# Query loads of six pairs of heads moved from SP's queue to ScalarE's, under a new order list

## The chip, the cores and the metric

The kernel runs on one core of a Trainium2 chip. The metric is the device time of one execution in microseconds, the median of several runs. A core has five engines that each execute their own instruction stream in order: TensorE (PE; its weight loads are listed as PEld), VectorE (DVE), ScalarE (ACT), GpSimd (POOL) and SyncE (SP). SP computes nothing: it issues DMA transfers. ACT and POOL can issue them too. The streams wait for each other by semaphores.

## The reference

Three layers follow each other. The first is causal attention over 2 batches of 8 heads with 576 positions and a head width of 64, with a bias from a running sum; the second a dense feed-forward layer (512 to 2048 to 512) on the 1152 tokens; the third sends each token to one of eight experts of width 1024.

```python
scores = scale * np.matmul(q, k.transpose(0, 1, 3, 2))
cum = np.cumsum(np.maximum(s, 0.0), axis=-1)
bias = -(cum[:, :, :, None] - cum[:, :, None, :])
scores = np.where(causal, -1000000000.0, scores + np.minimum(bias, 0.0))
attn = np.exp(scores - np.max(scores, axis=-1, keepdims=True))
attn = attn / (np.sum(attn, axis=-1, keepdims=True) + 1e-09)
x = np.matmul(attn, v)                    # then tokens x 512
...
h = x @ w_in
g = h * (1.0 / (1.0 + np.exp(-1.702 * h)))
x = g @ w_out
...
# the third layer: the expert of the largest gate logit, then w1, relu, w2, times its gate weight
```

## The kernel before

Operands are fp32 or are split into a high and a low 16-bit part, so that one product takes several matrix products.

**Pairs of heads.** Attention is done by pairs of heads: pair 0 to 7, called `x_` in the code (four of each batch). Their stages are interleaved with each other and with the beginning of the dense layer. For each pair:

- `qk_load` loads k and q of the two heads (288 KB each) to `kraw0`/`kraw1` and `qraw0`/`qraw1`, by the parity of `x_`, on SP (L630).
- `qk_T` transposes them on PE (L651) in the PSUM bank `MI`; ACT copies the results to `QK0` or `QK1` (L657). Two bias rows come from memory (`cum_d`, L640).
- `unit` goes through five query tiles, t = 0 to 4, with 64, 192, 320, 448 and 576 keys. PE computes scores (L680, the mask at L683; t = 0 is `first`, L694) in one of two PSUM score buffers, `SC0` and `SC1`, in turn. DVE takes the maximum (L724, L727), ACT the exponential to `pexp` (L736). The high part goes to `ph` by a copy (ACT L665 or DVE L667; L703 for t = 0), and POOL subtracts it for the low part (L749, L752). SP then issues a DMA transpose of `ph` to `PT` (L759). Tiles 0 and 1 share one, `PT01`, of 7 blocks of 128; `PT2`, `PT3` and `PT4` have 10, 14 and 18. For the last pair `PT3` and `PT4` are transposed in two halves each. Each of `PT` and `ph` exists once, so that the next pair's work on a tile waits for the last use of it.
- `av_unit` multiplies `PT` with `V` on PE (L779) into `AV`, DVE scales the result, PE transposes it (L803), and ACT (L806) and DVE (L808) write it to `xT`, the input of the dense layer.

**Around them.** Loads of v (L554), of weights of the dense layer (512 KB each to the `wraw` tiles: L320 for w_in, L323 for w_out) and of constants (L544, L545) are issued from SP too. The weights are converted from 64-bit floats on ACT, DVE and POOL (L352 to L369). The dense layer's first product is at L392 and L396 (by `dense`, `mm1`), its second at L425 and L426 (`mm2`). From about 130 us on the kernel computes the dense layer and then the experts.

**What sets the order.** A class `Plan` records operations, each with its engine, a function that emits it and what it depends on. `run` then emits them in the sequence of the table `ORDER`, a list of operation numbers (lines 23 to 133). So each engine's stream is that list, filtered by engine. `QS` maps the names `sp`, `pool`, `act` to the engines whose queues issue DMAs. The numbers of `dma`, `issue` and the like in the recorded operations are a planner's; `op` takes them, and the emission doesn't use them:

```python
        order = [n for n in ORDER if n0 <= n < self.done]
...
        for n in order:
            assert all(d < n0 or place[d] < place[n] for d in self.ops[n][2])
            self.ops[n][1]()
```

Of the kernel before, what the change touches and what calls it, by code (L numbers as in the profile page):

```python
# [198 lines left out]
def fused_kernel(ctx, tc, q, k, v, s, w_in, w_out, w_gate, w1, w2, cap, out):  # L199
    nc = tc.nc  # L200
# [20 lines left out]
    NBLK = 5  # L221
# [74 lines left out]
    QS = {"sp": nc.sync, "pool": nc.gpsimd, "act": nc.scalar}  # L296
    ISS = {"sp": 540.0, "pool": 1100.0, "act": 600.0}
# [176 lines left out]
    pl = Plan()  # L474
# [150 lines left out]
    def qk_load(x_):  # L625
        b, p = divmod(x_, NPR)
        i = x_ % NQR
# [1235 lines left out]
```

## Time and profile before

| | |
|---|---|
| median of 3 runs | 449.59 us (449.38 to 450.73) |
| the profiled execution | 453.84 us, its span 452.1 us |
| mean granted clock of PE over the span | 0.99 of full speed |
| busy share: PE, DVE, ACT, POOL | 94%, 75%, 59%, 28% |

The profile is of one execution, whose time (453.84 us) includes what lies around the span (452.1 us). Its times are counted from the start of the span. A line such as `L680` is a line of the kernel. SP's rows, marked `SPq`, show how long the engine was occupied with issuing a DMA, not how long the transfer took. "Idle before" in square brackets is the time in which an engine waited, and behind the arrow stands what ended that wait.

### The profile page before, as it was taken

How to read it: one execution, taken by the hardware profiler on the slowest of the kernel's cores; microseconds unless marked ns; L12 is line 12 of the kernel's file. 1: busy time of each engine (PE TensorE's matmuls, PEld its weight loads, DVE VectorE, ACT ScalarE, POOL GpSimd, SP SyncE). 2: the span in 40 equal slices, each digit the busy share in tenths (PEclk: the TensorE clock that was granted, in tenths of full speed). 3: DMA queues.
4: the chain of work that ended last, by engine and by line, in shares of the span. 5: the costliest groups of instructions: out<-in, count | busy, mean ns of one | idle time of the engine just before them, and what ended most of it. 6: DMA issues, size and time to landing. Idle time of an engine off the chain costs nothing.

```text
span 452.1 us, 10556 instructions
## 1 busy us (share of the span) xinstructions
PE 424.5 (94%) x3920; PEld 303.3 (67%) x3920; DVE 339.0 (75%) x909; ACT 268.5 (59%) x565; POOL 125.5 (28%) x147
## 2 busy tenths in 40 slices
PE   7878888999899999999999999999899999999992
PEld 6556566777555554555555665557899999999972
DVE  7688687898868787785565674878667778889971
ACT  2597789887344556454434443664355668868840
POOL 4365674687321212121110001500300113112122
PEclk9999999999989999999999999999999999999997
DMA  7899999999983423539900006795768789899901
GB/s 160 216 235 201 193 178 203 223 207 203 186 279 95 154 93 127 187 94 344 327 6 1 2 1 210 276 342 149 268 188 266 254 254 340 308 290 334 315 30 50
DMA packets 98000, 88.04 MB, mean 195 GB/s; under 512 B 65631, under 2 KB 76895, under 8 KB 97926
## 3 DMA queue, kind: packets, MB, share of 16 engines
q1 hardware_dynamic: 96068, 81.76, 67.7%
q0 software_dynamic: 1872, 5.52, 3.3%
q8 instruction: 32, 0.52, 0.5%
q14 instruction: 28, 0.23, 0.2%
HBM read 60.59 MB, written 14.17 MB: 165 GB/s over the span
## 4 chain that ended last, share of the span: by engine, by line
PE 54%; DMA 3%; DVE 2%; issue 2%; ACT 1%; POOL 1%; POOLq 0%; DVEq 0%
PE SC L425 8%; PE MX L392 5%; PE MI L392 4%; PE SC L426 4%; PE AV L1485 3%; PE AV L1486 3%; PE AV L1488 3%; PE MX L396 2%; PE MI L396 2%; PE AV L425 2%; PE MI L1454 2%; PE MI L1459 2%; PE MX L1454 2%; PE MI L1455 2%; PE MX L1459 2%
## 5 line engine op out<-in xcount | busy, mean ns | idle before, releaser
L425 PE MATMUL SC<-woH,gtH 128*128 128x512 f16 x212 | 63.5, 381 | 0.0
L392 PEld LDWEIGHTS <-wiH 128*128 128x128 f16 x384 | 37.7, 99 | 32.2 <-issue 3.2
L680 PE MATMUL SC<-QK 128*128 128x288 f32 (+3 forms) x160 | 52.6, 455 | 6.6 <-ACT pexp L736 5.4
L749 POOL TENSOR_TENSOR ph<-pexp,ph 128x512 f16<-128x512 f32 (+4 forms) x32 | 44.2, 1386 | 13.4 <-DVE ph L667 13.4
L392 PE MATMUL MI<-xT,wiH 128*128 128x384 f16 x216 | 44.2, 331 | 0.2 <-DVE th L402 0.2
L369 POOL TENSOR_TENSOR wiL<-wvi,wiH 128x512 f16<-128x512 f32 x16 | 19.9, 1244 | 87.6 <-ACT wiH L365 87.6
L425 PEld LDWEIGHTS <-gtH 128*128 128x128 f16 x276 | 26.6, 98 | 24.7 <-issue 0.3
L736 ACT ACTIVATE pexp<-SC,smA 128x192 f32<-128x192 f32 (+3 forms) x64 | 34.7, 573 | 12.1 <-DVE smA L724 8.4
L1372 DVE SCALAR_TENSOR_TENSOR woL<-wraw,woH 128x1024 f16<-128x1024 f32 x32 | 38.7, 1220 | 2.8 <-ACT woH L1370 2.8
L426 PE MATMUL SC<-woL,gtH 128*128 128x512 f16 x106 | 40.6, 383 | 0.0
L1372 DVE SCALAR_TENSOR_TENSOR wiL<-wraw,wiH 128x1024 f16<-128x1024 f32 x32 | 38.7, 1218 | 1.5 <-ACT wiH L1370 1.1
L680 PEld LDWEIGHTS SC<-QK 128*128 128x128 f32 x160 | 27.8, 196 | 16.3 <-ACT pexp L736 7.6
L392 PE MATMUL MX<-xT,wiH 128*128 128x384 f16 x168 | 35.1, 326 | 0.8 <-DVE th L402 0.8
L1370 ACT ACTIVATE wiH<-wraw 128x1024 f16<-128x1024 f32 x32 | 33.2, 1056 | 1.7 <-DMA wraw<-in_moe_w_dram 1.4
L1370 ACT ACTIVATE woH<-wraw 128x1024 f16<-128x1024 f32 x32 | 33.4, 1055 | 1.2 <-DMA wraw<-in_moe_w_dram 1.0
L408 DVE SCALAR_TENSOR_TENSOR gtH<-th,gtH 128x384 f16<-128x384 f32 x46 | 26.1, 574 | 10.4 <-ACT gtH L405 10.3
L1523 POOL DMA_INDIRECT out_dram<-x2R,small x9 | 10.7, 1190 | 81.2 <-ACT xT L1469 40.6
L1150 POOL DMA_INDIRECT xs_d<-x2R,small x9 | 10.4, 1150 | 80.9 <-DVE sqr L1245 42.7
L405 ACT ACTIVATE gtH<-th 128x384 f16<-128x384 f32 x46 | 23.3, 516 | 13.5 <-DVE th L402 8.6
L657 ACT ACTIVATE QK<-MI 64x288 f32<-64x288 f32 x57 | 24.3, 427 | 5.8 <-PE MI L651 5.0
L779 PE MATMUL AV<-V,PT 128*128 128x65 f16 (+1 forms) x640 | 23.7, 193 | 4.3 <-DMA PT<-ph 4.1
L396 PEld LDWEIGHTS <-wiL 128*128 128x128 f16 x192 | 18.6, 98 | 12.8
(347 smaller groups left out, 1080.7 us busy)
## 6 DMA issues: line engine op xcount, KB each, us to landing
wraw<-in_moe_w_dram SPq DMA_DIRECT2D x64, 512.0 KB, 5.8
wraw<-in_moe_w_in_dram SPq DMA_DIRECT2D x16, 512.0 KB, 6.5
wraw<-in_moe_w_out_dram SPq DMA_DIRECT2D x16, 512.0 KB, 5.2
xs_d<-x2R SPq DMA_DIRECT2D x16, 257.0 KB, 5.7
kraw<-in_k_dram SPq DMA_DIRECT2D x8, 288.0 KB, 4.9
qraw<-in_q_dram SPq DMA_DIRECT2D x8, 288.0 KB, 3.9
out_dram<-x2R SPq DMA_DIRECT2D x9, 256.0 KB, 7.4
x2R<-xs_d SPq DMA_DIRECT2D x8, 257.0 KB, 3.6
```

The source lines that it names most:

```text
L392: nc.tensor.matmul(ps, lhsT=whi[:, kc], rhs=xT[:, a, kc, cs], start=(kc == 0 and a == 0), stop=False)
L396: nc.tensor.matmul(ps, lhsT=wlo[:, kc], rhs=xT[:, 0, kc, cs], start=False, stop=(kc == KC - 1))
L408: pl.op("dve", t_dve(CN) + 65 * len(sums), lambda: nc.vector.scalar_tensor_tensor(out=gh[:, 1], in0=th, scalar=half, in1=gh[:, 0], op0=ALU ...
L425: nc.tensor.matmul(o, lhsT=gh[:, a, ts], rhs=whi, start=(fc == 0 and a == 0), stop=False)
L426: nc.tensor.matmul(o, lhsT=gh[:, 0, ts], rhs=wlo, start=False, stop=(fc == NFC - 1))
L657: pl.op("act", t_act(3 * TQ, False) + 130, lambda o=o, in_=in_, sc=sc: nc.scalar.activation(out=o, in_=in_, func=AF.Copy, scale=sc), r=[bk ...
L680: nc.tensor.matmul(o, lhsT=t_[:, 2 * r, i0:i0 + rows], rhs=t_[:, 2 * r + 1, j0:j0 + n], start=True, stop=(j0 + n <= i0))
L736: pl.op("act", t_act(wdt, False, 1), lambda o=o, e=e, r=r, nm=nm: nc.scalar.activation(out=e, in_=o, func=AF.Exp, bias=nm[:rows, r:r + 1]) ...
L749: pl.op(eng, (t_pool if eng == "pool" else t_dve)(n * T_), lambda rs_=rs_, e_=e_: e_.tensor_tensor(out=hl[:, rs_, 0:T_], in0=pe[:rows, rs_ ...
L779: nc.tensor.matmul(av[:, slot, r, 0:D + 1 - h_], lhsT=PT[t][:, r * (1 + 2 * t) + pb, :] if t else PTf[:, 64 * r:64 * r + P], rhs=rhs, star ...
L1370: pl.op("act", t_act(1024), lambda: nc.scalar.activation(out=dhi, in_=raw, func=AF.Copy, scale=SE), r=[rk], w=kh, rank=rank, after=after)
L1372: pl.op("dve", t_dve(1024) + 65, lambda: nc.vector.scalar_tensor_tensor(out=dlo, in0=raw, scalar=SE, in1=dhi, op0=ALU.mult, op1=ALU.subtra ...
```

## The change

In `qk_load` the loads of q for pairs 2 to 7 (the third to the eighth) are issued by ACT's queue. Those of k, and of q for pairs 0 and 1, stay on SP. The table `ORDER` is replaced by another one over the same operation numbers, which changes the streams of all engines in many places.

```diff
 ORDER = [
-    0, 2, 6, 8, 1, 7, 23, 13, 9, 3, 21, 4, 22, 14, 5, 29, 12, 19, 32, 20, 35, 33, 38, 10, 24, 30, 25, 41, 36, 31, 39, 37,
+    0, 1, 6, 15, 2, 8, 7, 21, 13, 9, 3, 22, 4, 23, 12, 5, 29, 20, 32, 19, 35, 33, 24, 38, 30, 34, 11, 25, 10, 41, 36, 31,
...
         for nm, src in (("k", k), ("q", q)):
-            t = raws[nm][i]
-            pl.op("sp", 0, lambda t=t, src=src: nc.sync.dma_start(
+            t, eng = raws[nm][i], "act" if x_ > 1 and nm == "q" else "sp"
+            pl.op(eng, 0, lambda t=t, src=src, eng=eng: QS[eng].dma_start(
                 out=t[:TQ], in_=src[b, 2 * p:2 * p + 2].rearrange("r (p c) d -> p r c d", c=S // TQ)),
-                w=[("raw", nm, i)], dma=820, after=[("vraw", NBLK - 1, 0)] if 1 <= x_ <= 2 else ())
+                w=[("raw", nm, i)], dma=820, issue=ISS[eng], after=[("vraw", NBLK - 1, 0)] if 1 <= x_ <= 2 else ())
```

Three places of the new order follow. In the rows a name such as `qraw0_113` is a tile and its number; the arrow points from source to destination.

ACT, at pair 2 (the copies to `QK1` are those of pair 3's keys and queries). Before:

```order
L657 ACTIVATE QK1_112<-MI_109 64x288 x2
L736 ACTIVATE pexp2_119<-SC0_105,smA_132 128x320 x2
L736 ACTIVATE pexp1_118<-SC1_106,smA_132 128x192
L806 ACTIVATE xT_90<-MX_110 128x320
L736 ACTIVATE pexp1_118<-SC1_106,smA_132 128x192
L657 ACTIVATE QK1_112<-MI_109 64x288 x2
L703 ACTIVATE ph01_122<-pexp0_117 128x64
L665 ACTIVATE ph01_122<-pexp1_118 128x2x192
L365 ACTIVATE wiH0_77<-wvi0_94 128x512
L736 ACTIVATE pexp3_120<-SC1_106,smA_132 128x448 x2
```

After:

```order
L657 ACTIVATE QK1_112<-MI_109 64x288 x2
L630 DMA qraw0_113<-in_q_dram 96x2x384
L736 ACTIVATE pexp1_118<-SC1_106,smA_132 128x192 x2
L665 ACTIVATE ph01_122<-pexp1_118 128x2x192
L657 ACTIVATE QK1_112<-MI_109 64x288
L806 ACTIVATE xT_90<-MX_110 128x320
L657 ACTIVATE QK1_112<-MI_109 64x288
L736 ACTIVATE pexp2_119<-SC0_105,smA_132 128x320 x2
L736 ACTIVATE pexp3_120<-SC1_106,smA_132 128x448
L630 DMA qraw1_114<-in_q_dram 96x2x384
L736 ACTIVATE pexp3_120<-SC1_106,smA_132 128x448
```

Both 192-wide exponentials now stand ahead of the 320-wide ones and of the copy to `xT`, a load of q stands ahead of them (pair 4), and another (pair 5) between the two 448-wide exponentials; the conversion at L365 and the copy at L703 have gone elsewhere.

SP, from the transposes of pair 0's last tile to those of pair 1's. Before:

```order
L630 DMA qraw1_114<-in_q_dram 96x2x384
L630 DMA kraw0_115<-in_k_dram 96x2x384
L759 DMA_TRANSPOSE PT4_129<-ph4_126 128x18x128
L759 DMA_TRANSPOSE PT2_127<-ph2_124 128x10x128
L630 DMA qraw0_113<-in_q_dram 96x2x384
L554 DMA vraw0_136<-in_v_dram 64x8x64 x2
L759 DMA_TRANSPOSE PT01_123<-ph01_122 128x7x128
L320 DMA wraw0_91<-in_moe_w_in_dram 128x4x256
L759 DMA_TRANSPOSE PT3_128<-ph3_125 128x14x128
L640 DMA QK1_112<-cum_d_73 2x2304
L759 DMA_TRANSPOSE PT4_129<-ph4_126 128x18x128
```

After:

```order
L630 DMA kraw0_115<-in_k_dram 96x2x384
L759 DMA_TRANSPOSE PT4_129<-ph4_126 128x18x128
L759 DMA_TRANSPOSE PT2_127<-ph2_124 128x10x128
L554 DMA vraw0_136<-in_v_dram 64x8x64
L759 DMA_TRANSPOSE PT01_123<-ph01_122 128x7x128
L320 DMA wraw0_91<-in_moe_w_in_dram 128x4x256
L640 DMA QK1_112<-cum_d_73 2x2304
L759 DMA_TRANSPOSE PT3_128<-ph3_125 128x14x128
L759 DMA_TRANSPOSE PT4_129<-ph4_126 128x18x128
```

Both loads of q are gone from this stretch, and one of the two pieces of v is issued later.

SP, at the end of the attention: the last rows of pair 6 and those of pair 7. Before:

```order
L759 DMA_TRANSPOSE PT01_123<-ph01_122 128x7x128
L323 DMA wraw1_92<-in_moe_w_out_dram 128x1024
L759 DMA_TRANSPOSE PT2_127<-ph2_124 128x10x128
L759 DMA_TRANSPOSE PT3_128<-ph3_125 128x14x128
L323 DMA wraw0_91<-in_moe_w_out_dram 128x1024
L759 DMA_TRANSPOSE PT4_129<-ph4_126 128x18x128
L759 DMA_TRANSPOSE PT2_127<-ph2_124 128x10x128
L759 DMA_TRANSPOSE PT01_123<-ph01_122 128x7x128
L320 DMA wraw2_93<-in_moe_w_in_dram 128x4x256
L759 DMA_TRANSPOSE PT3_128<-ph3_125 128x7x128 x2
L759 DMA_TRANSPOSE PT4_129<-ph4_126 128x9x128 x2
```

After:

```order
L759 DMA_TRANSPOSE PT4_129<-ph4_126 128x18x128
L323 DMA wraw0_91<-in_moe_w_out_dram 128x1024
L759 DMA_TRANSPOSE PT01_123<-ph01_122 128x7x128
L759 DMA_TRANSPOSE PT2_127<-ph2_124 128x10x128
L323 DMA wraw1_92<-in_moe_w_out_dram 128x1024
L759 DMA_TRANSPOSE PT3_128<-ph3_125 128x14x128
L759 DMA_TRANSPOSE PT4_129<-ph4_126 128x18x128
L759 DMA_TRANSPOSE PT01_123<-ph01_122 128x7x128
L759 DMA_TRANSPOSE PT2_127<-ph2_124 128x10x128
L320 DMA wraw2_93<-in_moe_w_in_dram 128x4x256
L759 DMA_TRANSPOSE PT3_128<-ph3_125 128x7x128 x2
L759 DMA_TRANSPOSE PT4_129<-ph4_126 128x9x128 x2
```

The two weight loads to `wraw0` and `wraw1` stand ahead of pair 6's PT01 and PT3; before, `wraw0` stood between pair 6's PT3 and PT4, and `wraw1` between its PT01 and PT2. Pair 7's PT01 now stands ahead of its PT2.

## Rows read from the trace of the kernel before

**Rows 1.** The page's first part: busy us, share of the span, instructions

```profile
PE 424.5 (94%) x3920; PEld 303.3 (67%) x3920; DVE 339.0 (75%) x909; ACT 268.5 (59%) x565; POOL 125.5 (28%) x147
```

**Rows 2.** Windows: stretch, its length, busy us by engine, granted clock, DMA share, GB/s

```profile
40.00:80.00 40.00, 32.84 (x389) 24.43 (x388) 31.32 (x77) 33.16 (x79) 25.35 (x27) 1.00 1.14 193
120.00:140.00 20.00, 18.13 (x148) 10.12 (x145) 15.48 (x33) 7.61 (x15) 4.07 (x14) 0.91 0.80 206
140.00:320.00 180.00, 178.96 (x1125) 100.52 (x1123) 127.50 (x331) 90.31 (x178) 23.40 (x22) 1.00 0.48 157
```

**Rows 3.** PE's waits: line, releaser, us in total, times, longest

```profile
PE SC L680 <- ACT pexp L736: 5.4, 7, 1.2
PE AV L779 <- DMA PT<-ph: 4.1, 3, 1.9
```

**Rows 4.** Timeline of PE, 42 to 71 us: start, duration, instruction, idle before

```profile
42.12 1.77 PE L680 MATMUL SC<-QK 128*128 128x448 f32 x4 [1.19 <-ACT pexp L736]
...
48.33 0.34 PE L694 MATMUL SC<-QK 128*64 128x64 f32 x4 [0.27 <-ACT xT L806]
...
49.49 0.92 PE L680 MATMUL SC<-QK 128*128 128x192 f32 x4
...
52.41 1.01 PE L779 MATMUL AV<-V,PT 128*128 128x65 f16 x28 [1.89 <-DMA PT<-ph]
...
66.97 0.44 PE L651 MATMUL MI<-identF,qraw 96*128 96x96 f32 x3 [0.79 <-DMA qraw<-in_q_dram]
...
70.21 1.77 PE L680 MATMUL SC<-QK 128*128 128x448 f32 x4 [1.24 <-ACT pexp L736]
```

**Rows 5.** Timeline of SP's issues, 29 to 62 us

```profile
29.75 6.97 SPq L759 DMA_TRANSPOSE PT<-ph  x2
36.81 0.54 SPq L630 DMA_DIRECT2D qraw<-in_q_dram  x1
37.41 1.37 SPq L554 DMA_DIRECT2D vraw<-in_v_dram  x2
...
45.75 3.20 SPq L759 DMA_TRANSPOSE PT<-ph  x1
...
61.35 0.58 SPq L630 DMA_DIRECT2D qraw<-in_q_dram  x1
```

**Rows 6.** Timeline of POOL, the last subtraction for pair 0's PT4

```profile
27.42 0.87 POOL L752 TENSOR_TENSOR ph<-pexp,ph 128x128 f16<-128x128 f32 x1
```

**Rows 7.** Timeline of ACT, 40 to 69 us

```profile
40.17 1.25 ACT L736 ACTIVATE pexp<-SC,smA 128x320 f32<-128x320 f32 x3 [0.76 <-DVE smA L724]
...
68.44 0.26 ACT L703 ACTIVATE ph<-pexp 128x64 f16<-128x64 f32 x1 [1.84 <-DMA PT<-ph]
```

**Rows 8.** Timeline of PE at the end of the attention

```profile
121.36 0.59 PE L425 MATMUL SC<-woH,gtH 128*128 128x512 f16 x2
...
124.04 0.50 PE L779 MATMUL AV<-V,PT 128*128 128x65 f16 x11 [1.87 <-DMA PT<-ph]
```

**Rows 9.** Timeline of SP's issues at the end of the attention

```profile
108.71 0.58 SPq L323 DMA_DIRECT2D wraw<-in_moe_w_out_dram  x1
109.47 4.79 SPq L759 DMA_TRANSPOSE PT<-ph  x1
...
118.07 1.22 SPq L759 DMA_TRANSPOSE PT<-ph  x1
```

**Rows 10.** Timeline of POOL, the subtraction for pair 7's PT3

```profile
114.97 0.91 POOL L749 TENSOR_TENSOR ph<-pexp,ph 128x384 f16<-128x384 f32 x1
```

**Rows 11.** Windows: the six us behind PE's wait at the end of the attention

```profile
124.00:130.00 6.00, 5.96 (x54) 3.42 (x55) 3.18 (x4) 2.56 (x5) 2.75 (x13) 0.72 1.05 301
```

**Rows 12.** Instructions of line L630 for q: duration in ns, least, median, most

```profile
L630 SPq DMA_DIRECT2D qraw<-in_q_dram x8: 444/557/1292, 1.7 to 89.2; - x8
```

**Rows 13.** Timeline of PE at the start of pair 0

```profile
19.20 1.24 PE L680 MATMUL SC<-QK 128*128 128x288 f32 x4 [0.61 <-ACT pexp L736]
...
20.74 0.47 PE L651 MATMUL MI<-identF,qraw 96*128 96x96 f32 x3
```

218 rows, old and new, of the table ORDER are left out of this document.

## The prediction, made before the result was known

> **What bounds the kernel now.** The table of busy times comes first: TensorE (PE) is busy 94% of the span [rows 1], so 452.1 - 424.5 = 27.6 us is all that any reordering can remove without removing work. The table by stage tells where that idle time lies [rows 2]. Between 140 and 320 us PE is busy 178.96 of 180, so whatever is won before 140 us is carried to the end: nothing there waits long enough to absorb it. From 40 to 80 us, inside the attention, PE is idle 40 - 32.84 = 7.16 us, and from 120 to 140 us, where the last pair of heads hands over to the feed-forward layer, 1.87 us, with a granted clock of 0.91. The list of PE's waits says what ends this idle time [rows 3]: the two score buffers, released by ScalarE's exponentials (ACT L736, 5.4 us in 7 waits), and the transposed probabilities that the DMA brings (PT<-ph, 4.1 us in 3 waits). Those are the terms that the change can move. VectorE, GpSimd and the dense part are not read further, since they are late nowhere that matters here.
>
> The profiled execution took 453.84 us (span 452.1); the median of the runs is 449.59. All durations below are of the profiled execution, the difference is formed against 453.84 and then carried to the median.
>
> **The change, part by part.** Six loads of queries (pairs 2 to 7) leave SP's queue and join ScalarE's (ACT's), and the whole order is new. PE executes the same matrix products before and after, so only waits can change.
>
> *a) The stall at pair 1's last transpose.* PE waited 1.89 us at 50.5 for PT4 of pair 1 [rows 4]. SP is the cause to look at: its ten issues from 29.75 to 45.75 follow each other with gaps of 0.2 us at most, direct loads between transposes [rows 5]. The change takes out ahead of that PT4 the q load (0.54 plus a gap of 0.06) and one of the two pieces of v (1.37 / 2 = 0.68). Ahead of pair 0's PT4 it takes out the q load (the row at 29.75 can begin no earlier than its data, and GpSimd finished those at 27.42 + 0.87 = 28.29 [rows 6], so at most 1.46). SP gains 0 to 2.76 us there. But PE reaches PT4 of pair 1 earlier as well, for the scores of pair 3 that stood ahead of it (0.34 + 0.92 [rows 4]) now stand behind: 1.26 us of cover is gone. Net: -1.26 to +1.5. I take 0.1: half of SP's gain (SP is back to back, but the data of its transposes may not all be ready sooner), less the lost cover.
>
> *b) The score buffers at pair 2.* PE waited 1.19 us at 42.12 for the exponentials of the 192-wide unit [rows 4]. On ACT the two 320-wide exponentials of the other buffer stood ahead of the first 192-wide one (the three took 1.25 us together [rows 7]), and the copy to xT ahead of the second. Now both 192-wide ones stand ahead of all that. The gain is 0 to 1.19; I take 1.1, because the two wide exponentials and the copy are together about as long as the wait. The q load that now stands ahead of the exponentials is charged in e).
>
> *c) Pair 3.* PE waited 0.79 us for q of that stage (66.97) and 1.24 us at 70.21 for the score buffer [rows 4]; behind the latter stands ACT's own wait of 1.84 us at L703, which overwrites the source of transpose PT01 of pair 3 and so waits for it until 68.44 [rows 7]. The q load now is issued from ACT while pair 2 is still computed, so the first wait should go. On SP the q load of 0.58 us ahead of that transpose is gone [rows 5], and a load of v is moved behind that transpose. Gain 0 to 2.03; I take 1.2, the larger wait, since part of it will be filled by the next thing that is late (the maximum of VectorE).
>
> *d) The end of the attention.* PE waited 1.87 us until 124.04 for PT3 of pair 7 [rows 8], whose first half was issued at 118.07, so issue to use is 5.97 us [rows 9]. Ahead of it the transpose PT4 of pair 6 took SP 4.79 us; the PT4 at 45.75 took 3.20 [rows 5, 9]. Before it a 512 KB weight load (108.71) stands directly between PT3 and PT4. The new order puts both weight loads ahead of earlier transposes, so I price PT4 at 3.20: 1.59 sooner, plus the load's 0.76 (108.71 to 109.47), 2.35 together. PT3's first half would then start at 115.7 (its data are ready at 115.88 at the latest [rows 10], so 0.2 may be lost) and land at 121.7. PE arrives at 124.04 - 1.87 = 122.17, or 0.59 earlier, since one group of L425 is moved behind: 121.6. The stall falls from 1.87 to about 0.1. Right behind the stall the granted clock fell: 0.72 over 124 to 130 us [rows 11], between the levels of 1.2 and 2.4 GHz, which cost 6 x 0.28 = 1.7 us. PE had waited 1.87 us just before. A wait of 1.89 at 50.5 was not followed by such a fall (1.00 from 40 to 80 us [rows 2]), so that the fall goes with the stall is an assumption. Gain 1.8 + 1.7 = 3.5, bounds 0 to 3.6.
>
> *e) What ACT pays.* No DMA is issued from ACT in the trace of before. The nearest row is the same load issued by SP: 0.444 / 0.557 / 1.292 us for least, median, most [rows 12]. ACT has time to spare (33.16 busy of 40 between 40 and 80 us [rows 2]), but its place in the loop of two score buffers is what PE waits for. Two of the six (pairs 2 and 7) stand beside copies that nobody waits for; four (pairs 3 to 6) stand between or ahead of exponentials or the copies that feed them. 4 x 0.557 = 2.2 us; bounds 0 (all covered by ACT's idle time) to 6 x 1.292 = 7.8. I take 2.2, the median, for it is the same kind of load.
>
> *f) The start.* In the new order the first 288-wide scores of pair 0 (19.20) stand behind the transposes of q of pair 1 (20.74) [rows 13], an operand that comes by DMA. 0.47 us of PE work stands ahead of the chain of exponentials: +0.5, bounds 0 to 1.5 (20.74 - 19.20, if the wait for q is as long as it looks).
>
> *Other moves.* The weight loads of the dense part, the biases and the constants move by a few places on SP, with PE's 7.16 us of idle time as cover; I cost them at nothing, but if that cover is gone each is worth its issue, 0.6 us.
>
> The Trainium skill ("DMA: Bandwidth & Descriptors", section "Issuing engines are not separate DMA queues") says that DMAs from any engine run on the same 16 engines and interleave, and that a second issuing engine saves only the issuing time. By that page the queue move would be worth six times 0.557 = 3.3 us of SP's time and no transfer would be faster. The trace of before cannot bear it out for ACT, since ACT issued no load there. The mechanism it would act by here is rival C.
>
> **The sum.** a) to c) lie on one loop, in which a wait removed at one buffer returns in part at the other; I count half: (0.1 + 1.1 + 1.2) / 2 = 1.2. Then d) 3.5, less e) 2.2, less f) 0.5: 2.0 us gained. 453.84 - 2.0 = 451.8 for a profiled execution; 449.59 - 2.0 = 447.6, rounded to **447.5 us** for the median.
>
> **The rivals.**
> B. *Both gains arrive in full and ACT hides its issues.* ACT's idle time of 6.84 us between 40 and 80 speaks for it [rows 2]. Then a) to c) give 2.4, d) 3.5, e) about 0.6, f) 0.5: 4.8 us, **445** (443.5 to 446).
> C. *The transfers, not the issuing, are the limit, and the change doesn't do what it says.* The DMA share is 1.14 from 40 to 80 us [rows 2], more than the sixteen engines' time by this count, and the issue of a PT4 takes 3.2 to 4.8 us, far longer than a direct load's 0.56, as if it were held by the transfers. If so, taking q off SP leaves the same bytes: PT lands when it did, q takes bandwidth from the transposes in flight, and the 4.79 of d) stays. The gain of a), c) and d) is gone, b) and e) cancel: **449.6** (448.6 to 450.6). Against it: at 109.47 the issue is slow only where a large load is directly ahead.
> D. *Slower: ACT pays.* The issue on ACT stands ahead of the exponentials that release the score buffers, PE waits, and every later exponential is late by as much. It decides from about 0.6 us for each of the six if the end stall stays (six times 0.6 = 3.6 against a gain of 1.2 from a) to c)): 449.59 - 1.2 + 3.6 + f) 0.5 = **452.5**, with 451 to 454 for issues of 0.4 to 0.9. The 1.292 at the top of the rows and the wait of 1.84 that ACT already suffers [rows 7] speak for it; that four of the six have other work before PE needs their exponentials speaks against it.
>
> **How the numbers follow.** The forecast has 0.40, with its own range 446 to 448.6; B 0.15; C 0.20; D 0.25. A measurement of this kernel can tell about 0.3% (1.35 us) from no change. Below 448.2 lie most of the forecast and B: 0.52 faster. Within 448.2 to 450.9 lie C and a little of the forecast's and D's edges: 0.23. Above: 0.25. The range must leave out no more than 2 in 10: from 444.0, inside B, to 451.8, inside D.
>
> **What the profile after would show.** Right: a wait for PT<-ph at the end of the attention under 0.4 us and a granted clock near 1.00 in the 6 us behind it; SP's PT4 of pair 6 near 3.2 us; q loads on ACT of about 0.56 us; PE's waits for L736 below 5 us in all. Wrong in d): PT4 of pair 6 near 4.8 us again, or the clock fallen as before (C). Wrong in e): q issues on ACT near 1.3 us, with PE's waits on L736 grown by 3 us or more (D). Wrong in f): PE's first 288-wide scores later than 20 us by more than 0.7. Any new wait of more than 2 us between 140 and 440 us would upset the carrying of the gain to the end.

## The result, and the profile after

The changed kernel takes 452.4 us (median of 20 runs) against 449.92 for the kernel before in the same comparison (20 runs): a ratio of 1.0053, 95% interval 1.0032 to 1.0074. It is slower by 0.53%, or 2.4 us. The forecast of 447.5 had the wrong sign, and the time lies outside the range.

The profiled execution of the changed kernel took 451.84 us (span 450.1). That this is 2.0 less than the profiled execution before says nothing of the change: that one lay 3.9 us above its own median (453.84 against 449.92), this one 0.6 below. A second profiled execution of the kernel before (run e1 below) took 451.84 too, span 450.1, to the digit the same. So the two kernels are compared below by stretches and by timed ratios, not by the two spans.

The first part of the page, and the table by stage with columns as in [rows 2]; the last stretch is one in which the clock fell:

```profile
PE 422.1 (94%) x3920; PEld 303.0 (67%) x3920; DVE 339.3 (75%) x909; ACT 269.4 (60%) x565; POOL 126.8 (28%) x147
```

```profile
40.00:80.00 40.00, 35.43 (x429) 26.83 (x427) 34.75 (x79) 33.81 (x79) 27.17 (x29) 0.99 1.11 201
120.00:140.00 20.00, 20.00 (x151) 11.33 (x150) 17.18 (x35) 9.51 (x19) 4.59 (x16) 1.00 0.76 204
140.00:320.00 180.00, 177.56 (x1116) 99.84 (x1115) 127.41 (x342) 90.17 (x178) 25.14 (x24) 1.00 0.48 154
30.00:42.00 12.00, 7.60 (x73) 5.68 (x70) 8.20 (x16) 6.01 (x14) 5.14 (x6) 0.72 1.10 198
```

PE's idle time from 40 to 80 us fell from 7.16 to 4.57 us, and that from 120 to 140 us from 1.87 to nothing, with a clock of 1.00 where it was 0.91 [rows 2]. Both were forecast. Two stretches lost. From 140 to 320 us, taken for a stretch that carries every gain to the end, the idle time rose from 1.04 to 2.44 us. And from 30 to 42 us PE was idle 4.4 of 12 us at a clock of 0.72, where the kernel before was idle 2.2 us at 1.00.

PE's waits (columns as in [rows 3]), the largest of the attention and then those behind it:

```profile
PE SC L680 <- ACT pexp L736: 3.1, 6, 1.1
PE AV L779 <- DMA PT<-ph: 2.9, 4, 1.5
PE AV L779 <- DVE V L620: 2.3, 1, 2.3
PE MX L803 <- DVE xT L808: 2.1, 3, 1.4
...
PE SC L1000 <- DVE th L995: 1.2, 2, 1.1
PE MI L983 <- DMA x2R<-xs_d: 0.4, 1, 0.4
```

The two waits of [rows 3] went from 9.5 us in all to 6.0. The third row (the product with V, 2.3 us at 35.93) was 0.2 us before. The last two rows stand at 306 to 320 us, where the kernel selects tokens for the experts (L983, L1000), and the kernel before has neither; it has one of 1.3 us a little later instead (L1454 for DVE's L1470).

### The profile page after: what moved, and what is told of

The parts are those of the page before. It is cut to its first block, busy times and chain, and to the rows that moved or that the text cites. A ratio compares the mean times of both kernels' runs of the same rounds, so it can differ in the third digit from the quotient of the medians.

```text
span 450.1 us, 10568 instructions
## 1 busy us (share of the span) xinstructions
PE 422.1 (94%) x3920; PEld 303.0 (67%) x3920; DVE 339.3 (75%) x909; ACT 269.4 (60%) x565; POOL 126.8 (28%) x147
## 4 chain that ended last, share of the span: by engine, by line
PE 66%; DMA 13%; DVE 7%; ACT 6%; issue 3%; SPq 2%; POOL 1%; POOLq 0%; ACTq 0%; DVEq 0%
PE SC L425 7%; PE MI L392 6%; PE MX L392 4%; PE SC L680 4%; DMA PT<-ph 4%; PE AV L1485 3%; PE SC L426 3%; PE AV L1486 3%; PE AV L1488 3%; DMA wraw<-in_moe_w_dram 3%; PE MI L396 3%; PE AV L425 3%; PE AV L779 2%; DMA x_d<-x2R 2%; PE MX L396 2%
## 5 line engine op out<-in xcount | busy, mean ns | idle before, releaser
L749 POOL TENSOR_TENSOR ph<-pexp,ph 128x512 f16<-128x512 f32 (+4 forms) x32 | 47.3, 1478 | 16.6 <-DVE ph L667 8.4
L736 ACT ACTIVATE pexp<-SC,smA 128x448 f32<-128x448 f32 (+3 forms) x64 | 34.9, 577 | 15.5 <-DVE smA L724 9.8
L369 POOL TENSOR_TENSOR wiL<-wvi,wiH 128x512 f16<-128x512 f32 x16 | 19.6, 1226 | 77.9 <-ACT wiH L365 71.2
L1523 POOL DMA_INDIRECT out_dram<-x2R,small x9 | 11.8, 1310 | 73.1 <-ACT x2R L1566 65.0
L779 PE MATMUL AV<-V,PT 128*128 128x65 f16 (+1 forms) x640 | 24.8, 194 | 5.2 <-DMA PT<-ph 2.9
L779 PEld LDWEIGHTS <-PT 128*128 128x128 f16 x640 | 22.9, 98 | 7.4 <-DMA PT<-ph 3.5
```

The costliest lines, as they stand in the source:

```text
L736: pl.op("act", t_act(wdt, False, 1), lambda o=o, e=e, r=r, nm=nm: nc.scalar.activation(out=e, in_=o, func=AF.Exp, bias=nm[:rows, r:r + 1]) ...
L749: pl.op(eng, (t_pool if eng == "pool" else t_dve)(n * T_), lambda rs_=rs_, e_=e_: e_.tensor_tensor(out=hl[:, rs_, 0:T_], in0=pe[:rows, rs_ ...
L779: nc.tensor.matmul(av[:, slot, r, 0:D + 1 - h_], lhsT=PT[t][:, r * (1 + 2 * t) + pb, :] if t else PTf[:, 64 * r:64 * r + P], rhs=rhs, star ...
```

## The experiments

Sixteen runs were made, in four groups on three chips: e1, e3, e4 and e5; e2, e6, e7 and e8; h1 to h4 on the same chip as the second group; i1 to i4. Each ratio is to the kernel before, run in the same group (medians 451.16, 451.39, 451.36 and 449.62). The interval of a ratio reaches 0.2 to 0.3% to either side, so single ratios that differ by 0.2% are not told apart, and what follows rests on several that agree, or on rows.

**The order against the queue.** e1 is the kernel before again; e2 the changed kernel again. e3 has the queue move under the old order, e4 the new order with all loads of q on SP, e5 the new order with pairs 2 and 3 back on SP.

> The kernel before, unchanged, for a second trace. My sum took the stall of 1.87 us at the end of the attention and the fall of the clock behind it (1.7 us) as if every execution had them; the profiled execution of before took 453.84 us, the median of 20 is 449.92. If the fall of the clock belongs to that execution alone, this trace has a time of 449 to 451 us, a granted clock of 0.99 or more over 120 to 130 us and no loss of more than 0.3 us to the clock there. Rival: it belongs to the kernel, and this trace shows a wait of 1.5 us or more at the end of the attention and a clock of 0.8 to 0.9 over 120 to 130 us, whatever its total.

> The changed kernel, unchanged, for a second trace and as the measure for the next two on this chip. Theory 1 (the changed order and queue make two waits of PE between 30 and 36 us, and the clock falls behind them in most executions): the waits of about 1.5 us for PT and 2.3 us for V (L620) stand here again, SP waits 5 us or more for q at PT2 of pair 0, and the mean granted clock of the runs lies 0.003 to 0.005 under that of before; 451.5 to 453 us. Theory 2 (chance of one execution): the waits or the fall of the clock are not seen again and the mean clock is that of before.

> The old order list, with the six loads of q on ACT's queue: the queue move alone. Theory 1 (what hurts is that SP's transposes wait for the landing of an ACT load, because all hardware DMAs take their completion semaphores in turn from the same eight, so that a DMA waits for the one eight places before it, and ACT's load lands late): here the transpose PT2 of pair 0 comes eight places behind the first of the ACT loads, so SP shows a wait for q there of 1 to 5 us, and the time is 451 to 455. Theory 2 (ACT pays for the issues in the loop of the score buffers): six issues of 0.33 us, 450.5 to 452, and no wait of SP for q. Theory 3 (the new order is what costs, the queue nothing): 449.2 to 450.6.

> The new order list with all loads of q on SP's queue: the order alone. Theory 1: SP's wait of 5.6 us at PT2 of pair 0 is gone, PT2 is issued before 23 us instead of 26.99, PE's waits of 1.48, 0.64 and 2.29 us at 31 to 36 us and the half clock behind them are gone; 445 to 449 us. Theory 2: the six issues of 0.33 us leave ACT, 450 to 451. Theory 3: the order costs as much as with the queue, 451.5 to 453, with the same waits at 31 to 36 us.

> The new order list, loads of q for pairs 2 and 3 back on SP, those for pairs 4 to 7 on ACT. Theory 1: only the first ACT load was eight places ahead of a transpose that was waited for, so this does as well as with all on SP, 445 to 449 us, with no wait of SP for q. Theory 2: four of the six issues remain on ACT, 451 to 452. Theory 3: 451.5 to 453.

```diff
-            t, eng = raws[nm][i], "act" if x_ > 1 and nm == "q" else "sp"
+            t, eng = raws[nm][i], "sp"
```

(This is e4; e5 has `x_ > 3`; e3 has the line of the changed kernel and the old table.)

Measured: e2 1.0047 [1.0027, 1.0067], e3 1.0017 [0.9985, 1.0050], e4 1.0031 [1.0005, 1.0057], e5 1.0020 [0.9989, 1.0052]. The new order loses time even with every load of q on SP, by an interval that excludes no change. The queue move alone is not told from nothing here. So, by these values, most of the loss is not ACT's, against rival D. In e2's trace the wait for V is there again (2.1 us) and SP's wait for q too (3.8), but PE's wait for PT at 31 to 34 us is not. The mean clock of e2's executions is 0.985 where the kernel before has 0.991, a difference that its first theory had nearly so; the section on the prediction comes back to that.

e1 speaks on step d). It took 451.84 us where 449 to 451 was expected, but the clock is what it was run for. Its row at the end of the attention, and two six-us stretches, the second right behind it:

```profile
123.08 0.50 PE L779 MATMUL AV<-V,PT 128*128 128x65 f16 x11 [2.27 <-DMA PT<-ph]
```

```profile
120.00:126.00 6.00, 3.73 (x38) 2.15 (x37) 3.75 (x9) 1.38 (x4) 0.79 (x1) 1.00 1.21 192
126.00:132.00 6.00, 6.00 (x60) 3.86 (x59) 5.31 (x11) 3.06 (x6) 1.96 (x13) 1.00 1.03 387
```

The same program waits 2.27 us there, more than the 1.87 of [rows 8], and the granted clock stays at 1.00. The fall to 0.72 of [rows 11] stands in that one execution and in none of the other seventeen traces.

**Mending what the trace after showed first.** The longest single wait of PE in the trace after is that of the product with V, 2.3 us; e6 moves the last two pieces of V ahead of other work on DVE, e7 does so with e5's queues. e8 is the kernel before with one thing from the new order, the weight loads of step d).

> The changed kernel with one edit on VectorE: the last two low halves of V (L620, from wiL and woL) stand ahead of the cast of pair 1's third tile and of two maxima, instead of behind them. Theory 1: PE's wait of 2.3 us for V at 33 to 36 us goes, the wait for PT remains (SP still waits for q at PT2 of pair 0), and the clock falls there more seldom: 1.5 to 3 us faster than the changed kernel on the same chip. Theory 2 (the wait is only handed on to the score buffers): within 0.7 us of the changed kernel, with a new wait of PE of over 1.5 us between 33 and 45 us.

> The same edit on VectorE, and the loads of q for pairs 2 and 3 back on SP. Theory 1: both waits go (PT2 of pair 0 is issued at about 22 us and the cast of pair 1's third tile no longer waits), 2.5 to 5 us faster than the changed kernel, 447.5 to 450 us; mean clock as in before. Theory 2: within 1 us of the changed kernel.

> The kernel before with one edit on SP: the weight load to wraw0 stands ahead of pair 6's PT01 and the one to wraw1 ahead of its PT3, as in the new order; all other streams are those of before. This is step d) of the prediction alone. If it holds, PT4 of pair 6 takes about 3.2 us instead of 4.8 on SP, PE's wait at the end of the attention falls from 1.9 to 2.4 us to under 0.7, and the time is 1 to 2.5 us less than before. Rival: SP issues without a gap there anyway and the transposes take as long in sum, the wait stays over 1.5 us and the time is that of before within 0.6 us.

e6, on DVE:

```diff
+L620 SCALAR_TENSOR_TENSOR V_130<-wiL_82,misc,V_130 128x8x64
+L620 SCALAR_TENSOR_TENSOR V_130<-woL_86,misc,V_130 128x8x64
 L667 CAST ph_124<-pexp_119 128x2x320
 L724 TENSOR_REDUCE smA<-SC_106 128x2
 L727 TENSOR_REDUCE smA<-SC_105 128x1
-L620 SCALAR_TENSOR_TENSOR V_130<-wiL_82,misc,V_130 128x8x64
-L620 SCALAR_TENSOR_TENSOR V_130<-woL_86,misc,V_130 128x8x64
```

e8, on SP, at pair 6:

```diff
 L759 DMA_TRANSPOSE PT_129<-ph_126 128x18x128
-L759 DMA_TRANSPOSE PT_123<-ph_122 128x7x128
-L323 DMA wraw_92<-in_moe_w_out_dram 128x1024
-L759 DMA_TRANSPOSE PT_127<-ph_124 128x10x128
-L759 DMA_TRANSPOSE PT_128<-ph_125 128x14x128
 L323 DMA wraw_91<-in_moe_w_out_dram 128x1024
+L759 DMA_TRANSPOSE PT_123<-ph_122 128x7x128
+L759 DMA_TRANSPOSE PT_127<-ph_124 128x10x128
+L323 DMA wraw_92<-in_moe_w_out_dram 128x1024
+L759 DMA_TRANSPOSE PT_128<-ph_125 128x14x128
 L759 DMA_TRANSPOSE PT_129<-ph_126 128x18x128
```

Measured: e6 1.0046 [1.0022, 1.0069], e7 1.0032 [1.0005, 1.0060], e8 0.9978 [0.9959, 0.9996]. Moving V forward gains nothing that shows. In e7 the wait for V is gone; in e6, too, but PE there waits for transposes in its place:

```profile
32.65 0.66 PE L779 MATMUL AV<-V,PT 128*128 128x65 f16 x16 [1.75 <-DMA PT<-ph]
34.51 1.38 PE L779 MATMUL AV<-V,PT 128*128 128x65 f16 x22 [0.92 <-DMA PT<-ph]
```

So the largest single wait was no cost that shows by itself; in e6 it was handed on. That theory fell. e8 gains 0.22%, 1.0 us, by an edit of SP's queue alone. PE is busy all of 120 to 130 us in it, at a clock of 1.00. Its PT4 of pair 6:

```profile
107.49 3.33 SPq L759 DMA_TRANSPOSE PT<-ph  x1
```

**Which half of the order loses.** The operations up to about 130 us ("attention") and the rest were put together from different tables. h1: attention of e8, rest of the new order. h2: attention of the new order with q on ACT, rest of the old. h3: as h2 with e7's edits. h4: e8 with the two 192-wide exponentials of pair 2, and the maximum on DVE that they need, ahead of the 320-wide ones: step b) by itself.

> Attention as in the kernel before with its two weight loads early (the run e8), but everything behind it (from about 130 us on: dense layer, routing, experts) in the new order. Theory 1 (the new order loses time behind the attention too: PE waits for the selection matrix, L1000, and for the rows of x2, L983, about 1.6 us together at 306 to 320 us in all traces of the new order and in none of the old): 1 to 2 us slower than e8 and these waits of 1.0 to 1.8 us are in its trace; about that of before, 451 to 452. Theory 2 (these waits are covered by a shorter tail): within 0.6 us of e8, 450 to 450.6.

> The changed kernel's attention (new order, q on ACT) and the rest in the old order. Theory 1: 1 to 2 us faster than the changed kernel, 451 to 452 when before is at 451.3, with no wait at L1000 over 0.3 us; what is left over before is the clock behind the waits at 30 to 36 us. Theory 2: as slow as the changed kernel, 452.8 to 453.6.

> The new attention mended (loads of q for pairs 2 and 3 on SP, the last two halves of V early on VectorE) and the rest in the old order. Theory 1: the gain of the end of the attention remains, the waits at 30 to 36 us and at 306 to 320 us do not: 449.5 to 451. Theory 2 (the new attention costs in other places too): 451.5 to 453.

> The run e8 with step b) of the prediction alone: in pair 2 the 192-wide maximum and exponentials stand ahead of the 320-wide ones on VectorE and ACT. If step b) holds, PE's wait of 1.0 to 1.2 us at 42 us goes and the time is 0.5 to 1.2 us under e8. Rival: the wait is handed on to the next score buffer and the time is that of e8 within 0.4 us.

h1 against e8, on DVE at the selection (many other rows differ too):

```diff
-L995 TENSOR_SCALAR th_89<-iotaW,small 128x128 x2
+L995 TENSOR_SCALAR th_89<-iotaW,small 128x128
+L1127 TENSOR_TENSOR small<-small,SC_106 128x8
 L1143 TENSOR_REDUCE small<-small 128x1
-L1127 TENSOR_TENSOR small<-small,SC_106 128x8
...
-L1134 SCALAR_TENSOR_TENSOR small<-small,misc 128x1
-L995 TENSOR_SCALAR th_89<-iotaW,small 128x128
 L1236 SCALAR_TENSOR_TENSOR srt<-SC_106,iota_66 128x8
...
 L1238 SCALAR_TENSOR_TENSOR srt<-srt_1920,srt 128x8
+L995 TENSOR_SCALAR th_89<-iotaW,small 128x128
...
+L1134 SCALAR_TENSOR_TENSOR small<-small,misc 128x1
 L1244 TENSOR_TENSOR sqr<-srt,iota_66 128x64
+L995 TENSOR_SCALAR th_89<-iotaW,small 128x128
```

h2 is the changed kernel with that put back (and the rest of the old order). h4 against e8, on ACT:

```diff
+L736 ACTIVATE pexp_118<-SC_106,smA 128x192 x2
 L736 ACTIVATE pexp_119<-SC_105,smA 128x320 x2
-L736 ACTIVATE pexp_118<-SC_106,smA 128x192
 L806 ACTIVATE xT<-MX 128x320
-L736 ACTIVATE pexp_118<-SC_106,smA 128x192
```

Measured: h1 1.0018 [0.9994, 1.0043], h2 0.9996 [0.9973, 1.0018], h3 0.9971 [0.9944, 0.9999], h4 0.9977 [0.9947, 1.0007]. With the old rest the changed attention costs nothing (h2 against e2: 0.51% less, with an interval of about 0.3% to either side); with the new rest e8's gain turns into a loss (h1 against e8, 0.40%). The two differences agree, and neither interval reaches zero: the loss sits behind the attention. h4 equals e8 within 0.35%: no gain of step b) alone shows, though this could hide the 0.5 to 1.2 us that were expected of it.

**The last group.** i1 is the changed kernel with only the selection's rows on DVE in the old sequence. i2 is h3 and i3 is h2, both with all q on SP; i4 is e8 again.

> The changed kernel with one edit on VectorE behind the attention: the second selection matrix of the first expert's rows (L995) follows the first at once, as in the old order, and the third stands three places behind the shift L1132 that precedes it. Theory 1 (VectorE's wait for PE at L1127, with the second L995 queued behind it, is what makes PE wait at L1000): PE's waits at L1000 fall from 1.2 to 1.4 us to under 0.3, and the time is 0.8 to 1.6 us less than the changed kernel's (ratio to before 0.9965 to 0.998 of the 1.0047 measured for it). Theory 2 (the wait is covered further on): ratio to before 1.004 to 1.006.

> The run h3 (mended new attention, old rest) with the last four loads of q also on SP: the queue move for pairs 4 to 7 alone, against h3 (ratio to before 0.9971). Theory 1 (these four cost and give nothing that can be measured): 0.995 to 0.9985. Theory 2 (the queue move helps SP's transposes): 0.9985 to 1.001. Theory 3 (it hurts): under 0.995.

> The run h2 (new attention, old rest) with all six loads of q on SP: the queue move alone in the new attention, against h2 (ratio to before 0.9996). Theory 1 (SP's transpose PT2 of pair 0 waits for ACT's load, which costs PE about 2 us at 31 to 34 us and sometimes the clock): 0.994 to 0.998. Theory 2 (what this wait costs is made up by the score buffers further on): 0.998 to 1.001.

> The run e8 again (the kernel before with its two weight loads early), to see whether its gain holds: if step d) of the prediction is real, ratio to before 0.995 to 0.9985; if it was chance, 0.9985 to 1.002.

i1 against the changed kernel, on DVE:

```diff
-L995 TENSOR_SCALAR th_89<-iotaW,small 128x128
+L995 TENSOR_SCALAR th_89<-iotaW,small 128x128 x2
 L1127 TENSOR_TENSOR small<-small,SC_106 128x8
...
 L1132 TENSOR_TENSOR small<-small 128x1
+L1134 SCALAR_TENSOR_TENSOR small<-small,misc 128x1
+L995 TENSOR_SCALAR th_89<-iotaW,small 128x128
...
-L995 TENSOR_SCALAR th_89<-iotaW,small 128x128
...
-L1134 SCALAR_TENSOR_TENSOR small<-small,misc 128x1
...
-L995 TENSOR_SCALAR th_89<-iotaW,small 128x128
```

Measured: i1 1.0022 [0.9991, 1.0053], i2 0.9978 [0.9954, 1.0001], i3 0.9969 [0.9945, 0.9992], i4 0.9992 [0.9966, 1.0018]. i3, the attention of the new order and nothing else of the change, is the fastest, with h3 close by: both beat the kernel before and the changed one. e8's gain of 0.22% came back as 0.08% in i4, a value that had been set down beforehand as speaking for chance. The two together give 0.17%, about 0.8 us, with an interval of 0.15% to either side, so that step d) has a gain is likely but barely shown.

## Where the time went

The three parts of the change by ratios, times 450 us: the new order of the attention -1.4 us (i3, 0.9969); the move of the loads in that order +1.2 (h2 less i3, 0.27%); the rest of the new order +2.3 (e2 less h2, 0.51%). They add up to e2's 1.0047 by the way they are formed, so the sum checks nothing. e4 is a check: the new order without the move should cost 2.3 - 1.4 = 0.9 us, 0.20%, and measured 0.31% [0.05, 0.57]. The terms come from different groups, so this account is only as good as the intervals; the first and the last term exclude zero, the second doesn't.

**The rest.** To compare the selection in all kernels I count from the start of the last L779 group, where the attention ends, and take the stretch from 180 us behind it to the first L1426. In these windows the second number is the stretch's length, the third PE's busy time. Of the kernel before:

```profile
309.55:330.78 21.23, 19.88 (x285) 18.84 (x284) 14.84 (x93) 9.54 (x29) 3.99 (x6) 1.00 0.57 183
```

of i4 (e8's program):

```profile
307.32:327.18 19.86, 19.86 (x287) 18.82 (x285) 14.81 (x93) 9.78 (x30) 3.99 (x6) 1.00 0.55 186
```

of the kernel after:

```profile
306.36:328.27 21.91, 20.15 (x282) 18.78 (x283) 15.30 (x96) 9.15 (x29) 3.73 (x4) 1.00 0.50 156
```

of h1 (the new rest behind e8's attention):

```profile
305.83:329.04 23.21, 20.61 (x285) 18.79 (x283) 16.49 (x98) 9.14 (x29) 3.73 (x4) 1.00 0.45 148
```

and of i1:

```profile
307.63:327.59 19.96, 19.70 (x284) 18.63 (x283) 15.31 (x94) 9.03 (x29) 3.73 (x4) 1.00 0.50 168
```

The old rest differs by group. It takes 20.8 to 21.9 us (21.3 on the mean) in the seven traces of the kernel before and the first three groups, which have a wait of 1.2 to 1.4 us there (PE L1454 for DVE L1470), and 19.6 to 19.9 us in the three of the last group, i4 with e8's program among them, which have not. So like goes with like. The new rest takes 21.9 to 23.2 us (22.6 on the mean) in the seven traces of the kernel after and the first three groups, 1.3 us more than the old. Behind the first L1426 the same traces take 121.7 us on the mean with the new rest and 121.2 with the old. The rows thus place some 1.8 us of the 2.3 in these two stretches. In the last group i1, which moves three rows of DVE, has 20.0 us, next to the old rest there. The timeline of DVE in the kernel after shows why:

```profile
314.92 0.35 DVE L995 TENSOR_SCALAR th<-iotaW,small 128x128 f32<-128x128 bf16 x1
317.03 0.16 DVE L1127 TENSOR_TENSOR small<-small,SC 128x8 f32<-128x8 bf16 x1 [1.76 <-PE MX L1459]
...
318.09 0.28 DVE L995 TENSOR_SCALAR th<-iotaW,small 128x128 f32<-128x128 bf16 x1
```

and that of PE in the same kernel:

```profile
316.23 1.12 PE L1000 MATMUL SC<-th,x2R 128*128 128x128 f32 x8
318.42 1.16 PE L1000 MATMUL SC<-th,x2R 128*128 128x128 f32 x8 [1.07 <-DVE th L995]
319.75 1.16 PE L1000 MATMUL SC<-th,x2R 128*128 128x128 f32 x8 [0.17 <-DVE th L995]
```

The same place in i1, DVE:

```profile
316.01 0.48 DVE L995 TENSOR_SCALAR th<-iotaW,small 128x128 f32<-128x128 bf16 x2
316.40 0.15 DVE L1127 TENSOR_TENSOR small<-small,SC 128x8 f32<-128x8 bf16 x1
```

and PE:

```profile
317.31 2.91 PE L1000 MATMUL SC<-th,x2R 128*128 128x128 f32 x24
```

In the changed order the second L995 stands behind L1127, which waits for PE 1.76 us, and PE in turn waits for L995. (Why L1127 waits so long isn't settled: the profile names L1459, which it doesn't read.) In the old order both L995 stand ahead of L1127. Putting them back makes the three groups of L1000 run without a gap. The wait at L1000 is 1.2 to 1.3 us in all seven other traces of the new rest and in none of the old. Timed, i1 loses 0.22% where the changed kernel lost 0.47 to 0.53%, about 1.2 us less. That alone is not shown: i1 ran on another chip than e2, and the interval of the difference, 0.37% to either side, includes zero. Part of the wait is handed on, too: behind the selection i1 has a wait that no other trace has, PE's L1426 for x2R, 0.9 us. Beside L1000 the traces of the new rest name one more wait, L983 for x2R, 0.4 us in after and 1.2 in h1 and e2. What makes the rest of the loss is not settled.

**The queue.** ACT itself paid little. Its six issues of q in the kernel after (least, median, most in ns):

```profile
L630 ACTq DMA_DIRECT2D qraw<-in_q_dram x6: 319/334/402, 18.4 to 89.3; - x6
```

One of them in ACT's timeline, between its copies:

```profile
20.03 0.43 ACT L657 ACTIVATE QK<-MI 64x288 f32<-64x288 f32 x1 [0.56 <-PE MI L651]
20.09 0.32 ACTq L630 DMA_DIRECT2D qraw<-in_q_dram  x1
20.47 0.43 ACT L657 ACTIVATE QK<-MI 64x288 f32<-64x288 f32 x1
```

The issue lies inside the running copy, and the next copy begins 0.01 us behind it; the other five issues lie inside a running instruction of ACT, too. What the move did was to hold up SP. The timeline of SP's issues in the kernel after:

```profile
21.03 0.27 SPq L640 DMA_DIRECT2D QK<-cum_d  x1
26.99 4.34 SPq L759 DMA_TRANSPOSE PT<-ph  x2
31.42 0.54 SPq L630 DMA_DIRECT2D kraw<-in_k_dram  x1
```

the row of SP's queue in its waits (us in total, times, longest):

```profile
SPq L759 <- DMA qraw<-in_q_dram: 5.6, 1, 5.6
```

and the timeline at the same place in i3:

```profile
22.09 7.46 SPq L759 DMA_TRANSPOSE PT<-ph  x2
29.64 0.54 SPq L630 DMA_DIRECT2D kraw<-in_k_dram  x1
```

A transpose on SP waits 5.6 us for a load of q that ACT issued, though it needs nothing from q. The semaphores in the trace tell why. The DMAs of SP and ACT signal their end on eight semaphores in turn (numbers 101 to 106, 108 and 110), and each first waits for the transfer that had its semaphore before, unless its engine has already done so. The load of q that ACT issued at 18.39 signals semaphore 102. The transpose PT2 stands eight places behind it in the program, has semaphore 102 as well, and so waits for the load. Each transfer raises the semaphore by 16; it reached 48, for a load of k, a piece of v and this load of q, at 26.92, and SP went on at 26.99. The load had taken 8.5 us.

SP's wait shows as 3.8 us in e2, 6.9 in e6, 5.4 in h2 and 6.3 in i1, and in none of the kernels that load q of pairs 2 and 3 on SP. SP's next load is 1.8 us late (31.42 for 29.64), and PE's waits for PT between 17 and 42 us are:

```profile
PE AV L779 <- DMA PT<-ph: 2.1, 2, 1.5
```
in the kernel after, and in i3
```profile
PE AV L779 <- DMA PT<-ph: 0.4, 1, 0.4
```

The same wait of PE is 2.7 us in e6, 2.4 in i1 and 0.9 in h2, but e2 has none, though SP waited there.

That the wait exists, and reaches PE in four of the five traces that have it, is shown; its worth is less sure. Four differences have the move cost something (h2 less i3 0.27%, e2 less e4 0.16%, the first measurement less e4 0.22%, e3 0.17%), but two share e4, and none is clear of its interval alone. e3's does not come from this wait. There, too, the transpose eight places behind ACT's first load has the load's semaphore (101), but SP came to it only at 26.5 us, from another transpose, and the load, issued at 19.38, had landed at 24.75. The loads of the last four pairs cost nothing that shows (h3 less i2, -0.07%).

## The prediction, step by step

The step *"whatever is won before 140 us is carried to the end"* is the one that failed. It was read from the trace of before, as if the change left the stretch alone, though "the whole order is new", and VectorE and the dense part were set aside as "late nowhere that matters here" (the trace of before has a wait of 1.3 us for VectorE at 323 us, L1454). PE was busy 178.96 of 180 us there [rows 2] in the old order; with 1.04 us idle, a new one could gain next to nothing there and lose much. What the new order does behind the attention stood in the sum at nothing, without a reason; it measured +2.3 us (e2 less h2, 0.51%), and the wait that the rows show is for VectorE (L995). The text named a "new wait of more than 2 us between 140 and 440 us" as a sign; it came as several small ones (1.1, 0.4, 0.2), too small for that sign.

*a)* The wait at pair 1's PT4 fell from 1.89 to 0.43 us (at 51.56), more than the 0.1 taken, within the bounds.

*b)* The wait at 42.12 [rows 4] is gone in the trace after, as forecast. In h4, which makes only this move, 0.67 us of it stays, 0.91 appears at L803 behind it, and the time is e8's. "I count half" was more than shows for this term: no gain of it alone was measured.

*c)* PE's waits for q and for the score buffer at pair 3 [rows 4] are gone, and L803 waits 1.44 us for DVE at 70.29 instead, the "next thing that is late (the maximum of VectorE)", only that it is DVE's copy L808. Of a) to c) and d) together i3 shows -1.4 us in the time, where 1.2 + 3.5 - 0.5 were summed.

*d)* SP did get through sooner and the stall went, as forecast. PT4 of pair 6, a weight load and PT3's first half in SP's timeline of the kernel after:

```profile
108.14 3.25 SPq L759 DMA_TRANSPOSE PT<-ph  x1
115.59 0.68 SPq L320 DMA_DIRECT2D wraw<-in_moe_w_in_dram  x1
116.43 1.22 SPq L759 DMA_TRANSPOSE PT<-ph  x1
```

and PE's row there, which had a wait of 1.87 us in [rows 8]:

```profile
121.89 0.49 PE L779 MATMUL AV<-V,PT 128*128 128x65 f16 x11
```

3.25 us against 3.20 taken and 4.79 before [rows 9], and no idle time ahead of L779. But the 1.7 us of clock in the term were one execution's, as e1 shows, and 1.8 us of stall were worth 0.4 to 1.0 us of time in i4 and e8 (0.08 and 0.22%). The reason given for PT4's 4.79 us, a load directly ahead, does not hold for every transpose (last section).

*e)* The price of 2.2 us for ACT was wrong both ways. 4 x 0.557 should have been near zero, since issues run beside ACT's own work; and the cost arose on SP. The Trainium skill ("DMA: Bandwidth & Descriptors", section "Issuing engines are not separate DMA queues") says that issuing from several engines saves only the time of issuing. The traces agree that the transfer is no faster: the first load of q took 8.5 us from ACT, and the loads of k and q that could be timed on SP in the kernel before took 3.9 to 5.4. The saving, 3.3 us of SP's issuing by the rows of before, was more than taken back at one place, where SP waited 5.6 us for ACT's load.

*f)* The first 288-wide scores came at 18.12 us, before the 19.20 of [rows 13]. The start was earlier as a whole, so the 0.5 us is neither shown nor refuted; nothing was lost there.

*The base.* The difference was carried from 453.84 to the median, which was right for all terms but the clock. The forecast of 451.8 for a profiled execution met 451.84, by chance: the losses behind the attention and a fallen clock from 30 to 42 us (12 x 0.28 = 3.4 us) are in it, and the sum had neither.

*The rivals.* B was right that ACT hides its issues, and far off in time. C said that PT4 stays at 4.79 us: refuted. D had the sign and nearly the time (452.5), by a mechanism that did not occur: PE's waits for L736 fell from 5.4 to 3.1 us. The range ended at 451.8, inside D; no case covered a loss behind the attention.

Still open: what makes the rest of the 2.3 us, and what the clock adds. Over all executions that were timed its mean is 0.990 to 0.991 in the kernel before and 0.985 to 0.987 in the changed one. Were all of this lost time, 0.005 x 450 = 2.3 us (an estimate) would be nearly the whole loss. Two things speak against it. i3 has 0.987 and is the fastest; and h1 loses 0.40% to e8 at 0.991 against 0.992. Within one kernel, 0.005 less clock went with about 0.4 us more time (an estimate from the scatter of 330 executions around the means of their kernels). So the clock is lower with the change, and that explains a part at most.

## What to carry to other kernels

When a change replaces a whole order, the stretches that were full before are where it can only lose: list what moved there too, engine by engine, and look for a row that waits and has a producer of the bottleneck's operand behind it. A wait seen in one profile is worth its length only if nothing else is late right behind it, and a clock that falls in one execution belongs to no edit until a second execution shows it at the same place: the fall at 124 us never came again, the one at 30 to 42 us did. Three parts that are differences of a chain of runs add up to the whole by themselves, so check them against a run outside the chain. Compare traces of one chip with each other. Before moving a DMA to another engine's queue, look at which semaphore it will share and who comes next on it.

## What the runs showed of the hardware

In one stretch the loads issued by ACT started later than the transfers on SP's queue. DMA queues of the kernel after from 18 to 21 us (queue: packets, MB, share of the sixteen engines; q1 carries SP's DMAs, q10 ACT's):

```profile
q1 hardware_dynamic: 992, 0.99, 105.0%
```

and from 21 to 27 us:

```profile
q1 hardware_dynamic: 1264, 0.64, 65.3%
q10 hardware_dynamic: 238, 0.34, 43.7%
```

ACT had issued loads at 18.39 and 20.09, yet its queue moved nothing before 21 us, while SP's moved 0.99 MB. The Trainium skill ("DMA: Bandwidth & Descriptors", section "Queues, rings and completion order") has packets of different queues take turns. In these three us none of ACT's came through; whether the turns or a late start made that, no run here tells apart.

How long SP is occupied with issuing one and the same transpose varies, and no simple rule for it comes out of the rows. PT4 of pair 6 took 4.79 us directly behind a 512 KB load [rows 9] and 3.25 and 3.33 us without one directly ahead (after, e8). But PT3 of pair 6 took 3.28 us in the kernel before, where PT2 stands directly ahead of it, and 2.31 us in the kernel after, directly behind a 512 KB load (2.28 in e8, likewise):

```profile
105.38 3.28 SPq L759 DMA_TRANSPOSE PT<-ph  x1
```

(before), and

```profile
105.59 2.31 SPq L759 DMA_TRANSPOSE PT<-ph  x1
```

(after).

The granted clock does not fall at a fixed place in a program, and yet not just anywhere. In two profiles of the kernel before it was 0.72 at 124 to 130 us [rows 11] and 1.00 throughout 120 to 132. In one of the changed kernel it was 0.72 at 30 to 42 us (above); in another, e2, it was 1.00 there and 0.72 over 46 to 52 and over 80 to 86 us. The stretch from 30 to 42 us in e2, and then in e6, h2 and i1 (columns as in [rows 2]):

```profile
30.00:42.00 12.00, 9.76 (x125) 7.77 (x126) 10.70 (x22) 9.51 (x21) 7.32 (x8) 1.00 1.08 183
```

```profile
30.00:42.00 12.00, 9.30 (x84) 6.87 (x82) 8.14 (x15) 7.41 (x17) 5.18 (x7) 0.72 1.15 186
30.00:42.00 12.00, 8.76 (x81) 6.53 (x81) 8.12 (x16) 7.17 (x17) 5.14 (x6) 0.72 1.07 211
30.00:42.00 12.00, 7.48 (x79) 5.66 (x77) 7.59 (x15) 5.71 (x15) 5.14 (x6) 0.72 1.32 187
```

The kernel after, e6, h2 and i1 are just the four traces in which SP's wait for q reaches PE as waits for PT of 0.9 to 2.7 us; e2, where it does not, keeps 1.00. In the other fourteen traces the clock there is 1.00, except for 0.86 in e5. So this fall goes with the queue move wherever PE was held up by it.
